# Attention with a mixture of experts on one core: the second sweep's first expert takes its last chunk after both groups, and GpSimd scales half of the weights

## The chip, the core and the metric

One of the eight cores of a Trainium2 chip runs the whole program. The metric is the device time of one execution in microseconds: 979.92 us for the kernel before (median of three, 979.89 to 981.65).

## What is computed

Causal attention with a decay (4 batches, 8 heads, 576 tokens, head size 64) makes x, 2304 tokens by 512. Four experts of two layers (512 to 1024 to 512) then run on every token and are summed with normalised weights p. All of it is in float32.

```python
scores = q @ k.T / 8 + cum[:, None] - cum[None, :]   # cum: running sum of log f; causal
x = softmax(scores) @ v                              # per head, joined to [2304, 512]
out = sum(p[:, e:e+1] * (relu(x @ w1[e]) @ w2[e]) for e in range(4))
```

## The kernel before

**Work.** Tokens are cut into nine chunks of 256. Each expert has eight slabs of 128 hidden features; a slab holds a piece of the first layer's weights (columns 0 to 511 of a tile) and of the second layer's (512 to 1023). A group g is half an expert, four slabs; a step (s, g, c, ps) is two of its slabs on one chunk in one sweep: 24 matmuls of 128x256 in `l1` (L859), a gate, and 12 of 128x512 in `l2` (L891), whose sums end in `gather` (L910, L914). Every value is split into a high and a low part and three products are added.

**Sweeps.** `SWEEPS` lists the chunks of each expert. The first sweep takes what attention has finished early. The second, in float16 pairs, takes chunks 1, 2, 3, 4 for experts 0 and 1, chunks 2 to 4 for expert 2 and 3 to 4 for expert 3: steps 28 to 79 of 80. Chunks 5 to 8 come last, in the class `Big`. In a sweep the groups come one after the other, and a group does all its chunks before the next group starts.

**Attention in between.** The heads of attention are 64 (pair of heads, half of the tokens): `qk_pe` (s, L540), `qk_min` and `qk_exp`, `tr_pe` (t, L632), `av_pe` (o, L682), `spread` (b, L600). They are issued in small pieces between the parts of the steps. `marks` and `pace` spread them by estimated costs so that a chunk is there `LEAD` steps before the first step that uses it; if it isn't, `upto(need[cur.c])` issues all that is missing at once. Chunk 4 needs all the heads of batch 0's second half. Before a chunk's first step in the second sweep, `x_scale` finds its largest value (xmax, L253, then topx on PE, L192 and L213), and `narrow` makes its float16 pair y (L411 on ACT, L412 on DVE).

**Weights.** `w_load` brings a slab into one of three tiles wr. `w_split` makes the pair of a slab in the second sweep: for each half k, ACT scales and rounds (L826) and DVE subtracts (L827). It is called when a group's last chunk releases two slabs, and splits the two that lie six slabs ahead (L1259 to L1262). In the second sweep there is room for twelve slabs. Each pair is also stored for later (wd). `w_peek` reads the next expert's weights for their largest value, one piece a step (pk, L277).

**Order.** Below the startup a scheduler fixes the order of each engine's instructions when the program is built; each engine runs its list in order and waits where an input is late. POOL (GpSimd) also makes pieces of q and k of every head (L488, L496, L502) and spreads the reciprocals (rb, L590).

Of the kernel before, what the change touches and what calls it, by code (L numbers as in the profile page):

```python
# [12 lines left out]
AF = mybir.ActivationFunctionType  # L13
ALU = mybir.AluOpType
# [11 lines left out]
SWEEPS = (  # L26
    ((0,), (0,), (0, 1), (0, 1, 2)),
    ((1, 2, 3, 4), (1, 2, 3, 4), (2, 3, 4), (3, 4)),
)
# [5 lines left out]
LAST = (5, 6, 7, 8)  # L35
# [40 lines left out]
def fused(ctx: ExitStack, tc: tile.TileContext, qk, v, f, probs, w, out):  # L76
    nc = tc.nc
# [105 lines left out]
    def at_step(n, f):  # L183
        later.setdefault(n, []).append(f)
# [47 lines left out]
    def behind(f):  # L232
        if prev is None:
            f()
            return
        with tc.issue_after(prev.last.ins):
            f()
# [32 lines left out]
    def w_peek(e, i):  # L270

        n, k = divmod(i, 2)
        t = pk_p.tile([128, 512], F32, tag="pk", name=f"pk{e}_{i}")
        nc.sync.dma_start(out=t, in_=w[8 * e + n, :, 512 * k : 512 * k + 512])
        at_step(
            step + 1,
            lambda: nc.vector.tensor_reduce(  # L277
                out=wmax[:, k, n, e : e + 1], in_=t, op=ALU.max, axis=AX.X, apply_absolute_value=True
            ),
        )  # L280
# [57 lines left out]
    def weigh(e, c):  # L338

        k = min(c, LAST[0])  # L340
        if (e, k) in weighed:
            return
        weighed.add((e, k))
        assert ("w", e) in known and ("x", k) in known
        o = slice(2 * c, 2 * c + 2) if c < LAST[0] else slice(2 * LAST[0], 2 * LAST[-1] + 2)
        nc.gpsimd.tensor_scalar(
            out=scg[:, e, o],
            in0=prob[:, o, e],
            scalar1=wun[:, e : e + 1],
            scalar2=xun[:, k : k + 1],  # L350
            op0=ALU.mult,
            op1=ALU.mult,
        )
# [52 lines left out]
    def narrow(c):  # L406

        y_tiles(c)
        sc = xsc[:, c : c + 1]
        x = xh[c].bitcast(F32) if c in WIDE else xf[c]  # L410
        nc.scalar.activation(out=yh[c], in_=x, func=AF.Copy, scale=sc)  # L411
        nc.vector.scalar_tensor_tensor(  # L412
            out=yl[c], in0=x, scalar=sc, in1=yh[c], op0=ALU.mult, op1=ALU.subtract
        )
        if c in WIDE:
            nc.vector.scalar_tensor_tensor(
                out=yl[c], in0=xl[c].bitcast(F32), scalar=sc, in1=yl[c], op0=ALU.mult, op1=ALU.add
            )
# [364 lines left out]
    wh, wl, wraw = {}, {}, {}  # L783
    NS = len(SWEEPS) * E * (FF // 128)

    def w_load(n):
        if n < NS and n not in wraw:
            wraw[n] = wr_p.tile([128, 1024], F32, tag="wr", name=f"wr{n}")
            nc.sync.dma_start(out=wraw[n], in_=w[n % 32])
# [3 lines left out]
    def w_pair(name):  # L793
        t = w_p.tile([128, 2, 1024], F16, tag=("wh", "wl")[len(pairs) % 2], name=name)
        pairs.append(t)
        return t

    def w_split(n):
        if n >= NS:
            if n % 2 == 0:  # L800
                big_split((n - NS) // 2)
            return
        w_load(n)
        r = wraw.pop(n)
        if n < 32:
            wh[n] = w_p.tile([128, 1024], F32R, tag="wh", name=f"wh{n}")
            wl[n] = w_p.tile([128, 1024], F32R, tag="wl", name=f"wl{n}")
            nc.scalar.activation(out=wh[n], in_=r, func=AF.Copy)
            eng = nc.vector if n in W_DVE else nc.gpsimd
            for a in (0, 512):  # L810
                z = a + 512
                eng.tensor_tensor(
                    out=wl[n][:, a:z],
                    in0=r[:, a:z],
                    in1=wh[n][:, a:z].bitcast(F32),
                    op=ALU.subtract,
                )
        else:
            e = n % 32 // 8
            assert ("w", e) in known  # L820
            t = w_pair(f"w{n}")
            wh[n], wl[n] = t[:, 0], t[:, 1]
            for k in range(2):
                c = slice(512 * k, 512 * k + 512)
                sc = wsc[:, e, k : k + 1]
                nc.scalar.activation(out=wh[n][:, c], in_=r[:, c], func=AF.Copy, scale=sc)  # L826
                nc.vector.scalar_tensor_tensor(  # L827
                    out=wl[n][:, c],
                    in0=r[:, c],
                    scalar=sc,  # L830
                    in1=wh[n][:, c],
                    op0=ALU.mult,
                    op1=ALU.subtract,
                )
            at_step(step + 2, lambda: nc.sync.dma_start(out=wd[n - 32], in_=t))
        w_load(n + 1)
        w_load(n + 2)
        w_load(n + 3)
# [141 lines left out]
    def big_split(p):  # L980
        if p >= 16:
            return
        r = wr_p.tile([128, 2, 512], F32, tag="wr", name=f"wr{NS + p}")
        nc.sync.dma_start(
            out=r, in_=w[2 * p : 2 * p + 2, :, :512].rearrange("n p c -> p n c")
        )
        bw[p] = [w_pair(f"bw{p}_{k}") for k in range(3)]
        for k in range(2):
            nc.sync.dma_start(out=bw[p][k], in_=wd[2 * p + k])
        part = lambda b: r[:, b[0], 256 * b[1] : 256 * b[1] + 256]  # L990
        t = late.x.tile([128, 4, 256], F32, tag="wt", name=f"wt{p}", bufs=2)
        w_of = lambda b: part(b) if type(b) is tuple else t[:, b - 1, :]
        for k, a, z, op in SUMS:
            nc.gpsimd.tensor_tensor(out=t[:, k - 1, :], in0=w_of(a), in1=w_of(z), op=op)  # L994
        f = t.rearrange("p k n -> p (k n)")
        hi, lo = bw[p][2][:, 0], bw[p][2][:, 1]
        nc.scalar.activation(out=f, in_=f, func=AF.Copy, scale=wsc[:, p // 4, 0:1])
        nc.scalar.activation(out=hi, in_=f, func=AF.Copy)  # L998
        for a in (0, 512):
            z = a + 512  # L1000
            nc.gpsimd.tensor_tensor(out=lo[:, a:z], in0=f[:, a:z], in1=hi[:, a:z], op=ALU.subtract)  # L1001

    class Big:
# [81 lines left out]
    steps = [  # L1085
        Step(s, g, c, ps)
        for s, sets in enumerate(SWEEPS)
        for g in range(8)
        for c in sets[g // 2]
        for ps in range(2)  # L1090
    ]

    done_at = {}
    for n, (j, _) in enumerate(heads):
# [37 lines left out]
    def upto(n):  # L1132
        nonlocal at
        while at < n:
            asteps[at][1]()
            at += 1
# [14 lines left out]
    def pace(n):  # L1151
        for (n0, c0), (n1, c1) in zip(marks, marks[1:]):
            if n <= n1:
                goal = c0 + (c1 - c0) * (n - n0) / (n1 - n0)
                break
        else:
            goal = cost[-1]
        m = at
        while m < len(asteps) and cost[m + 1] <= goal:
            m += 1  # L1160
        upto(m)
# [45 lines left out]
    prev, step = None, 0  # L1207
# [13 lines left out]
    for n in range(len(steps) + 1):  # L1221
        step = n
        cur = steps[n] if n < len(steps) else None
        for f_ in later.pop(n, ()):
            behind(f_)
        for e, first_ in enumerate(PEEK):
            if 0 <= n - first_ < 16:
                w_peek(e, n - first_)
            if n == first_ + 17:
                a_, b_ = w_scale(e)  # L1230
                behind(a_)
                at_step(n + 3, b_)
        if cur is not None:
            if cur.c not in used:
                used.add(cur.c)
                upto(need[cur.c])
            for c, m in TURN:
                if n >= m and c not in yh and ("x", c) in known:
                    narrow(c)
            if cur.s == 1:  # L1240
                assert cur.c in yh
                weigh(cur.g // 2, cur.c)
            for q in range(4):
                cur.l1(q)
                pace(n + q / 8)
            cur.gate()
        else:
            upto(len(asteps))
            chunks.close()
            late.h = late.enter_context(tc.tile_pool(name="h", bufs=8, side="right"))  # L1250
            for e in range(E):
                weigh(e, LAST[0])
            big = [Big(p) for p in range(16)]
            big[0].l1()
        if prev is not None:
            for q in range(4):
                prev.l2(q)
                pace(n + (q + 4) / 8)
            if prev.c == SWEEPS[prev.s][prev.g // 2][-1]:  # L1259
                base = prev.w0 + 6  # L1260
                w_split(base)
                w_split(base + 1)  # L1262
        prev = cur

    for p in range(16):
# [49 lines left out]
```

## Time and profile before

| what | us |
|---|---|
| median of three | 979.92 |
| the profiled execution, its own time | 980.82 |
| its span, first to last instruction | 978.6 |
| PE busy | 944.8 |
| DVE, ACT, POOL busy | 709.4, 471.0, 341.9 |

The span is what the profile covers; the profiled execution's own time is 2.2 us longer than it and 0.9 us above the median. PE is the matrix engine, DVE the vector engine, ACT the scalar engine, POOL GpSimd, SP the queue that issues the transfers. A busy PE need not be a PE at its full rate. The second sweep runs from about 238 to 661 us.

### The profile page before, as it was taken

The numbers are of one execution on the slowest core, as the hardware profiler recorded it, in microseconds if no ns is written. First come the engines' busy times: TensorE is split into PE (matmuls) and PEld (weight loads), VectorE is DVE, ScalarE is ACT, GpSimd is POOL, SyncE is SP. The second block draws the span as 40 slices with busy tenths as digits, with TensorE's granted clock in tenths as the row PEclk, the third lists the DMA queues.
The fourth block names the chain that finished last, engine by engine and source line by source line (L and its number), as shares of the span: only waits on it lengthen the run. The fifth ranks groups of instructions, "written<-read, shape, count | busy, mean of one in ns | idle before, by whom it ended". The sixth has DMA issues, their size and how long they took to land.

```text
span 978.6 us, 15658 instructions
## 1 busy us (share of the span) xinstructions
PE 944.8 (97%) x5695; PEld 647.8 (66%) x5695; DVE 709.4 (72%) x1485; ACT 471.0 (48%) x931; POOL 341.9 (35%) x400
## 2 busy tenths in 40 slices
PE   5799999999997999999999999999999999999998
PEld 4699999898765877777777777764444444444443
DVE  5768767877878897677966785568766766676665
ACT  6767465466467765446745564364222322231110
POOL 4766776343133422213222121386224223320000
PEclk9999999999999899999999999999999999999999
DMA  6456644485623293333922192044222312121002
GB/s 220 138 167 220 221 148 149 127 285 194 225 79 103 78 398 111 95 108 123 388 90 62 56 365 74 28 151 151 86 65 86 108 66 79 51 65 44 0 1 86
DMA packets 49772, 129.41 MB, mean 132 GB/s; under 512 B 5700, under 2 KB 8320, under 8 KB 49696
## 3 DMA queue, kind: packets, MB, share of 16 engines
q1 hardware_dynamic: 49696, 128.42, 38.6%
q8 instruction: 45, 0.74, 0.3%
q14 instruction: 31, 0.25, 0.1%
HBM read 106.75 MB, written 21.65 MB: 131 GB/s over the span
## 4 chain that ended last, share of the span: by engine, by line
PE 83%; DVE 5%; POOL 4%; DMA 3%; ACT 3%; issue 2%; SPq 0%; ACTq 0%; POOLq 0%; DVEq 0%
PE l L859 19%; PE l L891 18%; PE y L1074 17%; PE m L1016 14%; PE s L540 5%; PE t L632 5%; PE o L682 5%; DMA raw<-in_qk 1%; POOL wt L994 1%; DMA wr<-in_w 1%; POOL bw L1001 1%; PE b L600 1%; POOL rx L974 1%; DVE p L554 1%; DMA pk<-in_w 1%
## 5 line engine op out<-in xcount | busy, mean ns | idle before, releaser
L859 PE MATMUL l<-y,w 128*128 128x256 f16 x1248 | 162.4, 273 | 0.6 <-DVE y L412 0.6
L1074 PE MATMUL y<-bw,hh 128*128 128x512 f16 x512 | 151.8, 379 | 1.3 <-ACT hh L1042 1.3
L1016 PE MATMUL m<-rh,bw 128*128 128x512 f16 x448 | 139.1, 379 | 0.4 <-ACT rh L975 0.4
L569 ACT ACTIVATE p<-p,nm 128x576 f32<-128x576 f32 (+2 forms) x160 | 96.0, 600 | 88.2 <-DVE nm L554 87.6
L859 PEld LDWEIGHTS <-w 128*128 128x128 f16 x1248 | 117.4, 98 | 29.1 <-issue 6.8
L914 DVE SCALAR_TENSOR_TENSOR acc<-y,scg,acc 128x512 f32<-128x512 f32 x120 | 89.4, 749 | 59.8 <-PE y L1074 59.0
L891 PE MATMUL l<-w,gh 128*128 128x512 f16 x416 | 126.5, 380 | 1.4 <-ACT gh L872 0.9
L1016 PEld LDWEIGHTS <-bw 128*128 128x128 f16 x672 | 65.8, 98 | 79.6 <-issue 0.7
L488 POOL CAST q<-raw 64x320 fp32r<-64x320 f32 (+1 forms) x56 | 24.9, 445 | 266.6 <-PE s L540 203.8
L1001 POOL TENSOR_TENSOR bw<-wt,bw 128x512 f16<-128x512 f32 x32 | 37.2, 1184 | 174.0 <-ACT bw L998 174.0
L1074 PE MATMUL y<-bw,hl 128*128 128x512 f16 x256 | 96.5, 379 | 0.0
L554 DVE CUSTOM_DVE_ANT_0 p<-s,mask 128x288 f32<-128x288 f32 (+2 forms) x160 | 75.5, 477 | 23.8 <-PE s L540 22.9
L540 PE MATMUL s<-hi 128*128 128x384 f32 (+1 forms) x192 | 77.2, 405 | 15.2 <-DVE hi L502 8.8
L1074 PEld LDWEIGHTS <-hh 128*128 128x128 f16 x512 | 50.0, 98 | 62.0 <-ACT hh L1042 1.8
L632 PE MATMUL t<-ident,p 128*128 128x128 f32 x480 | 86.2, 287 | 4.1 <-ACT p L569 3.9
L1033 DVE TENSOR_TENSOR u<-m,u 128x512 f32<-128x512 f32 x96 | 65.6, 689 | 28.0 <-PE m L1016 27.0
L649 DVE TENSOR_TENSOR ptl<-t,pth 128x320 fp32r<-128x320 f32 (+2 forms) x120 | 65.5, 552 | 27.6 <-ACT pth L642 27.0
L1016 PE MATMUL m<-rl,bw 128*128 128x512 f16 x224 | 84.9, 379 | 0.0
L642 ACT ACTIVATE pth<-t 128x384 fp32r<-128x384 f32 (+2 forms) x120 | 58.0, 498 | 43.0 <-PE t L632 38.8
L891 PE MATMUL l<-w,gl 128*128 128x512 f16 x208 | 78.4, 379 | 0.0
L873 DVE SCALAR_TENSOR_TENSOR gl<-l,gh 128x512 f16<-128x512 f32 (+1 forms) x80 | 54.8, 686 | 30.4 <-ACT gh L872 29.9
L1042 ACT ACTIVATE hh<-u 128x512 f16<-128x512 f32 x64 | 39.5, 627 | 76.5 <-DVE u L1033 76.4
(136 smaller groups left out, 2069.8 us busy)
## 6 DMA issues: line engine op xcount, KB each, us to landing
wr<-in_w SPq DMA_DIRECT2D x80, 512.0 KB
pk<-in_w SPq DMA_DIRECT2D x64, 256.0 KB
wd<-w SPq DMA_DIRECT2D x32, 512.0 KB
bw<-wd SPq DMA_DIRECT2D x32, 512.0 KB
raw<-in_qk SPq DMA_DIRECT2D x16, 896.0 KB
raw<-in_qk SPq DMA_DIRECT2D x12, 512.0 KB
vr<-in_v SPq DMA_DIRECT2D x16, 320.0 KB
out<-acc SPq DMA_DIRECT2D x16, 256.0 KB
```

The source lines that it names most:

```text
L540: nc.tensor.matmul(out=ps[:, at : at + z - a], lhsT=lhsT, rhs=rhs, start=(m == 0), stop=(m == 1),)
L554: nc.vector.tensor_tensor_reduce(out=pt[:, a:z], in0=ps, in1=mask[:, m0 + a : m0 + z], scale=-0.125, scalar=BIG if n == 0 else nm[:, col : ...
L569: nc.scalar.activation(out=pt[:, :w_], in_=pt[:, :w_], func=AF.Exp, scale=-1.0, bias=self.nmax[hh][:, c : c + 1], accum_out=self.ssum[:, h ...
L632: nc.tensor.transpose(ps[:, at : at + 128], self.p[hh, it][:, TOK0[jt] : TOK0[jt] + 128], ident)
L642: nc.scalar.activation(out=self.pt[hh][0][:, a0 : a0 + at - first], in_=ps[:, first:at], func=AF.Copy)
L649: nc.vector.tensor_tensor(out=lo[:, a0 + first : a0 + at - first], in0=ps[:, 2 * first : at], in1=hi[:, a0 + first : a0 + at - first].bitc ...
L859: nc.tensor.matmul(out=self.l1p[:, fi, :], lhsT=lhsT, rhs=rhs[:, k, :], start=(k == 0 and m == 0), stop=(k == 3 and m == 2),)
L891: nc.tensor.matmul(out=l2[tt], lhsT=lhsT, rhs=rhs, start=(self.ps == 0 and fi == 0 and m == 0), stop=(self.ps == 1 and fi == 1 and m == 2),)
L914: nc.vector.scalar_tensor_tensor(out=acc[c][:, tt, :], in0=ps, scalar=sc, in1=acc[c][:, tt, :], op0=ALU.mult, op1=ALU.add,)
L1016: nc.tensor.matmul(out=ps, lhsT=lhsT[:, o], rhs=rhs[:, k, :], start=(k == 0 and i == 0), stop=(k == 1 and i == 2),)
L1033: nc.vector.tensor_tensor(out=out, in0=a, in1=z, op=op)
L1074: nc.tensor.matmul(out=ps, lhsT=lhsT, rhs=rhs, start=(fi == 0 and m == 0), stop=(fi == 1 and m == 2),)
```

## The change

Two edits. The order of the steps: group 0 of the second sweep's first expert leaves out chunk 4, group 1 does chunks 1, 2 and 3, and then group 0 and group 1 do chunk 4. The table `ends` says which step now triggers which `w_split`, so that the slabs of both groups stay. And in the second sweep the second layer's half (k = 1) of each slab is scaled in place by POOL, rounded by ACT and subtracted by POOL; DVE no longer touches it.

```diff
             for k in range(2):
                 c = slice(512 * k, 512 * k + 512)
                 sc = wsc[:, e, k : k + 1]
+                if k == 1:
+                    nc.gpsimd.tensor_scalar(
+                        out=r[:, c], in0=r[:, c], scalar1=sc, scalar2=None, op0=ALU.mult
+                    )
+                    nc.scalar.activation(out=wh[n][:, c], in_=r[:, c], func=AF.Copy)
+                    nc.gpsimd.tensor_tensor(
+                        out=wl[n][:, c], in0=r[:, c], in1=wh[n][:, c], op=ALU.subtract
+                    )
+                    continue
                 nc.scalar.activation(out=wh[n][:, c], in_=r[:, c], func=AF.Copy, scale=sc)
...
+    behind_1 = [t for t in steps if (t.s, t.g, t.c) == (1, 0, LAST[0] - 1)]
+    for t in behind_1:
+        steps.remove(t)
+    at_1 = next(n for n, t in enumerate(steps) if (t.s, t.g, t.c) == (1, 1, LAST[0] - 1))
+    steps[at_1:at_1] = behind_1
+    ends = {
+        t.w0: t for t in steps if t.c == SWEEPS[t.s][t.g // 2][-1] and t not in behind_1
+    }
+    for t in steps:
+        if t.s == 1 and t.c == LAST[0] - 2 and (t.g, t.ps) in ((0, 0), (1, 0)):
+            ends[32 + 2 * t.g] = t
...
-            if prev.c == SWEEPS[prev.s][prev.g // 2][-1]:
-                base = prev.w0 + 6
-                w_split(base)
-                w_split(base + 1)
+            for w0, t in ends.items():
+                if t is prev:
+                    w_split(w0 + 6)
+                    w_split(w0 + 7)
```

The order, as the scheduler leaves it. In a name such as l2_1_0_3_0_1 stand sweep, group, chunk, ps and the token half; in s0_2_1_0_3_0 batch, pair of heads, half, head, tile. The last number of a name is a buffer's.

PE, before, where group 0 ends with chunk 3:

```order
L891 MATMUL l2_1_0_3_0_1_4311<-w35_3755,gl1_0_3_1_4293 128x512
L632 MATMUL t0_1_1_1_0_3225<-ident_111,p0_1_1_1_4_3020 128x128
L632 MATMUL t0_1_1_1_0_3225<-ident_111,p0_1_1_1_3_3019 128x128
L632 MATMUL t0_1_1_1_0_3225<-ident_111,p0_1_1_1_4_3020 128x128
L632 MATMUL t0_1_1_1_1_3262<-ident_111,p0_1_1_1_4_3020 128x128
L632 MATMUL t0_1_1_1_1_3262<-ident_111,p0_1_1_1_2_3018 128x128
L632 MATMUL t0_1_1_1_1_3262<-ident_111,p0_1_1_1_3_3019 128x128
L632 MATMUL t0_1_1_1_1_3262<-ident_111,p0_1_1_1_4_3020 128x128
L540 MATMUL s0_2_1_0_3_0_3277<-hi0_2_1_0_3025 128x512
L540 MATMUL s0_2_1_0_3_0_3277<-kl0_2_1_0_2863,q2_0_113 128x512
```

From there to the first matmul of chunk 4 the list holds 188 matmuls, all of them attention's.

PE, with the change, at the same place:

```order
L900 MATMUL l2_1_0_3_0_1_4309<-w35_3753,gl1_0_3_1_4294 128x512
L868 LDWEIGHTS w38_4324
L868 MATMUL l1_1_1_1_1_4419<-y1_2362,w38_4324 128x256
L540 MATMUL s0_2_1_1_4_0_3514<-hi0_2_1_1_3206 128x288
L540 MATMUL s0_2_1_1_4_0_3514<-kl0_2_1_1_3036,q2_1_114 128x288
L868 LDWEIGHTS w38_4324
L868 MATMUL l1_1_1_1_1_4419<-y1_2362,w38_4324 128x256
```

Group 1 goes on behind group 0's last row, and attention's rows stand between its own.

PE, with the change, where group 1 ends with chunk 3:

```order
L900 MATMUL l2_1_1_3_0_1_4853<-w39_4332,gh1_1_3_1_4837 128x512
L900 LDWEIGHTS gh1_1_3_1_4837
L900 MATMUL l2_1_1_3_0_1_4853<-w39_4332,gh1_1_3_1_4837 128x512
L900 LDWEIGHTS gl1_1_3_1_4838
L900 MATMUL l2_1_1_3_0_1_4853<-w39_4332,gl1_1_3_1_4838 128x512
L540 MATMUL s1_0_1_1_3_0_4182<-hi1_0_1_1_3911 128x512
L540 MATMUL s1_0_1_1_3_0_4182<-kl1_0_1_1_3723,q2_1_114 128x512
L213 MATMUL topx4_172<-ux4_173,ones_r_126 128x1
```

From the last l2 row to the first matmul of chunk 4 the list now holds 32 matmuls.

POOL, before, from the reciprocals of one pair of heads to those of the last pair that chunk 4 needs (rb0_3_1):

```order
L590 COPY rb0_2_1_3509<-rs0_2_1_3181 128x384
L488 CAST q2_0_113<-raw1_0_1_3552 64x320
L496 TENSOR_TENSOR kl1_0_1_0_3550<-raw1_0_1_3552,hi1_0_1_0_3708 64x576
L502 TENSOR_TENSOR hi1_0_1_0_3708<-raw1_0_1_3552,hi1_0_1_0_3708 64x320
L488 CAST q2_1_114<-raw1_0_1_3552 64x320
L496 TENSOR_TENSOR kl1_0_1_1_3713<-raw1_0_1_3552,hi1_0_1_1_3893 64x576
L502 TENSOR_TENSOR hi1_0_1_1_3893<-raw1_0_1_3552,hi1_0_1_1_3893 64x320
L590 COPY rb0_3_1_3839<-rs0_3_1_3544 128x384
```

POOL, with the change, the end of the same stretch:

```order
L488 CAST q2_0_113<-raw1_0_1_3561 64x320
L831 TENSOR_TENSOR w42_5236<-wr42_4338,w42_5236 128x512
L496 TENSOR_TENSOR kl1_0_1_0_3559<-raw1_0_1_3561,hi1_0_1_0_3718 64x576
L502 TENSOR_TENSOR hi1_0_1_0_3718<-raw1_0_1_3561,hi1_0_1_0_3718 64x320
L827 TENSOR_SCALAR wr43_4872<-wr43_4872,wsc_120 128x512
L827 TENSOR_SCALAR wr44_4880<-wr44_4880,wsc_120 128x512
L831 TENSOR_TENSOR w43_5244<-wr43_4872,w43_5244 128x512
L827 TENSOR_SCALAR wr45_5242<-wr45_5242,wsc_120 128x512
L488 CAST q2_1_114<-raw1_0_1_3561 64x320
L496 TENSOR_TENSOR kl1_0_1_1_3723<-raw1_0_1_3561,hi1_0_1_1_3911 64x576
L502 TENSOR_TENSOR hi1_0_1_1_3911<-raw1_0_1_3561,hi1_0_1_1_3911 64x320
L590 COPY rb0_3_1_3877<-rs0_3_1_3553 128x384
```

Between head pieces of q and k now stand pieces of the weights (wr, w), and rb0_3_1 is behind them.

## Rows read from the trace of the kernel before

**Rows 1.** The page: PE over the whole span, and the granted clock in 40 slices.

```profile
PE 944.8 (97%) x5695; PEld 647.8 (66%) x5695; DVE 709.4 (72%) x1485; ACT 471.0 (48%) x931; POOL 341.9 (35%) x400
...
PEclk9999999999999899999999999999999999999999
```

**Rows 2.** Windows: span, busy us of each engine (instructions), granted clock, DMA share, GB/s.

```profile
285.20:328.90 43.70, 34.77 (x198) 27.42 (x197) 35.13 (x104) 33.21 (x72) 19.18 (x22) 0.92 0.27 87
...
315.90:328.90 13.00, 10.02 (x47) 8.46 (x48) 9.77 (x31) 9.96 (x21) 7.30 (x8) 0.74 0.12 30
...
237.90:328.90 91.00, 82.07 (x523) 62.34 (x523) 74.00 (x194) 59.81 (x125) 30.39 (x35) 0.96 0.38 128
...
328.90:656.00 327.10, 326.92 (x2321) 244.11 (x2321) 241.99 (x556) 180.39 (x358) 91.96 (x108) 1.00 0.44 155
...
340.00:620.00 280.00, 279.83 (x1988) 210.26 (x1986) 211.38 (x493) 157.96 (x321) 62.91 (x72) 1.00 0.47 167
```

**Rows 3.** Windows, the same columns, four microseconds each.

```profile
316.00:320.00 4.00, 1.66 (x12) 1.61 (x12) 3.66 (x8) 2.93 (x5) 2.04 (x2) 0.92 0.00 0
...
320.00:324.00 4.00, 4.00 (x15) 3.12 (x14) 3.48 (x15) 2.29 (x7) 1.25 (x3) 0.50 0.26 82
```

**Rows 4.** Timeline of PE: start, us, instruction, count, [idle before <- releaser].

```profile
315.34 0.55 PE L600 MATMUL b<-ident,rb 128*128 128x128 f32 x3
...
318.34 0.27 PE L192 MATMUL topx<-ident,xmax 128*1 128x128 f32 x1 [2.45 <-DVE xmax L253]
...
328.92 2.78 PE L859 MATMUL l<-y,w 128*128 128x256 f16 x24 [0.56 <-DVE y L412]
```

**Rows 5.** Lines by form, PE, 340 to 620 us: count | busy us, mean ns.

```profile
L859 PE MATMUL l<-y,w 128*128 128x256 f16 x912 | 119.6, 273 | 0.0
...
L891 PE MATMUL l<-w,gh 128*128 128x512 f16 x296 | 90.1, 380 | 0.0
...
L891 PE MATMUL l<-w,gl 128*128 128x512 f16 x149 | 56.4, 379 | 0.0
```

**Rows 6.** Chain that ended last, two merged pieces: start us, us, what.

```profile
340.05 2.62 PE l L859 x24
...
349.74 1.29 PE l L891 x6
```

**Rows 7.** Timeline of DVE around the wait for chunk 4.

```profile
317.07 1.21 DVE L253 TENSOR_REDUCE xmax<-xf 128x1 f32<-128x1024 f32 x1
...
326.76 0.56 DVE L554 CUSTOM_DVE_ANT_0 p<-s,mask 128x384 f32<-128x384 f32 x1 [2.17 <-PE s L540]
...
327.62 1.25 DVE L412 SCALAR_TENSOR_TENSOR y<-xf,xsc,y 128x1024 f16<-128x1024 f32 x1
```

**Rows 8.** Lines by form, DVE, whole span.

```profile
L277 DVE TENSOR_REDUCE wmax<-pk 128x1 f32<-128x512 f32 x64 | 43.4, 678 | 13.2 <-DMA pk<-in_w 13.2
...
L873 DVE SCALAR_TENSOR_TENSOR gl<-l,gh 128x512 f16<-128x512 f32 x52 | 35.6, 686 | 16.6 <-ACT gh L872 16.3
...
L914 DVE SCALAR_TENSOR_TENSOR acc<-l,scg,acc 128x512 f32<-128x512 f32 x48 | 35.5, 744 | 2.8 <-PE l L891 2.6
```

**Rows 9.** One line at a time, L826 and L827: count, duration min/median/max, starts.

```profile
L826 ACT ACTIVATE w<-wr,wsc x64: 705/709/723, 202.4 to 581.3; 128x512 f16<-128x512 f32 x64
...
L827 DVE SCALAR_TENSOR_TENSOR w<-wr,wsc,w x64: 700/746/1521, 204.3 to 582.7; 128x512 f16<-128x512 f32 x64
```

**Rows 10.** Lines by form, POOL, whole span.

```profile
L1001 POOL TENSOR_TENSOR bw<-wt,bw 128x512 f16<-128x512 f32 x32 | 37.2, 1184 | 174.0 <-ACT bw L998 174.0
...
L488 POOL CAST q<-raw 64x320 fp32r<-64x320 f32 x32 | 14.5, 452 | 231.3 <-PE s L540 180.5 <-DMA raw<-in_qk 19.6 <-DMA pk<-in_w 13.8
...
L590 POOL COPY rb<-rs 128x384 f32<-128x384 f32 x16 | 11.4, 710 | 34.1 <-DVE rs L588 33.8
```

**Rows 11.** One line, L976: the same DVE form beside a busy POOL.

```profile
L976 DVE SCALAR_TENSOR_TENSOR rl<-rx,xsc,rh x8: 740/1342/1724, 647.0 to 665.8; 128x512 f16<-128x512 f32 x8
```

**Rows 12.** Waits, whole span: us in total, times, longest us.

```profile
POOL q L488 <- PE s L540: 208.7, 30, 18.9
```

## The prediction

> **What bounds the kernel now.** I read the page's first table first: PE is busy 944.8 of 978.6 us [rows 1]. What it has to do doesn't change, so a gain can only come from the 34 us in which it stands, or from time in which it is busy but slow. Part of these lie at the program's start and end, where the change moves nothing. The granted clock, in the same rows, drops once in the middle, so there I asked for windows. From 285.2 to 328.9 us PE is busy 34.8 of 43.7 us, and the next 327 us have no hole [rows 2]. The hole is the wait for chunk 4: between the last l2 row of chunk 3 and the first l1 row of chunk 4 the order has 188 matmuls of attention and nothing of the experts. It ends with 2.45 us in which PE waits for the chunk's largest value, and 0.56 us in which it waits for y [rows 4]. In 316 to 324 us the granted clock is 0.92 and then 0.50, the lower of its two levels (1.2 of 2.4 GHz) [rows 3], right behind that idle time. Then comes the DVE timeline: the y of chunk 4 is the end of a line of small DVE instructions that starts at the xmax of 317.07 [rows 7].
>
> **First part: the order of the steps.** Nothing is added on PE; six steps move from behind chunk 4 to before it.
>
> What is a packed microsecond worth? In 340 to 620 us PE is full and mixes both kinds of work. An l1 matmul takes 2.62/24 = 0.109 us and an l2 matmul 1.29/6 = 0.215 us in the chain [rows 6]. The 912 and 445 of them [rows 5] take 99.4 + 95.7 = 195.1 us, so the other 1988 - 1357 = 631 matmuls [rows 2] get 84.9 us, 0.135 us each. The hole holds 198, two of them l1: 196 x 0.135 + 0.2 = 26.6 us if packed. It takes 43.7. So **17.1 us** are lost there: the idle time, the low clock, and ends of matmuls that nothing overlaps.
>
> How much of it comes back? A step is 24 x 0.109 + 12 x 0.215 = 5.2 us, six are 31.2 us, more than the hole needs. But they don't reach its end. In the new order, behind the last b rows of chunk 4's heads, there remain 5 l1, 24 l2 and 43 small matmuls: 0.5 + 5.2 + 5.8 = 11.5 us. In the trace it takes 13.0 us from there to y, with DVE busy 9.8 [rows 2]. DVE's list in the changed order has four instructions more in that stretch, a gl, a pk and two acc: 0.69 + 0.68 + 2 x 0.74 = 2.9 us [rows 8]. If DVE's waits stay, y comes after 15.9 us; the largest, 2.17 us for a score matmul [rows 7], fell into the slow clock, and with 1 us of waits in all it is 13.6. So PE still waits 2.1 to 4.4 us for chunk 4; I take **3.2**. I expect no drop of the clock, since l2 rows now stand where PE idled 2.45 us.
>
> Then the density. From the sweep's start to chunk 4 the time becomes 91.0 - 17.1 + 31.2 + 5.2 = 110.3 us (3.2 for chunk 4, and 2 for what this paragraph says). DVE's work there goes from 74.0 us [rows 2] up by six gl, six acc and six pk (4.1 + 4.5 + 4.1), by the first halves of six more slabs (6 x 0.746 = 4.5 [rows 9]) and down by four second halves (3.0): 88.2 us, or 80%. That is DVE's share in the hole (35.1 of 43.7), where head waited for head; in 340 to 620 us it is 75% and PE doesn't wait. I allow **2 us** for short waits, between nothing and the 7 us of the first rival. Behind chunk 4, 40 steps instead of 46 carry the same heads, and DVE has about 207 us of work in 296, 70% (242 less six steps' 12.7, less 4.5 of halves done earlier, less 24 second halves' 17.9), against 74% before. No hole opens there by DVE.
>
> **Second part: half of the weights on POOL.** Removed: 32 DVE subtractions of 0.746 us, 24 us. DVE isn't on the path outside of the hole, so this alone is worth nothing; in the hole it is the 3.0 us above. ACT keeps its 32 instructions of 0.71 us. Added: 32 subtractions on POOL, whose nearest row is bw, the same shape and types, 1.18 us; and 32 scalings with one tensor input. The trace has none of this size. Below, the cast of 64x320 takes 0.45 us and longer rows can't take less; above, the two-input row takes 1.18; the copy of 128x384 takes 0.71 [rows 10], and by its columns 512 make 0.95, which I take. That is 2.1 us a slab, 68 us of POOL in all. POOL is busy 92.0 of 327.1 us behind chunk 4 [rows 2]; with 20 slabs 134 of 296. What hides it: weights are split two or more steps (10 us) before their use, against about 3 us for POOL, ACT, POOL. If that cover goes, PE waits in l2. Queued behind POOL's new rows are the pieces of q and k and rb0_3_1, on which the next score matmuls and chunk 4 wait. A tile wr is held longer by these 2 us, so loads and stores on SP start later by as much; I cost that at nothing while PE's steps lie further ahead.
>
> **The sum.** 17.1 - 3.2 - 2.0 = 11.9 us. The profiled execution would go from 980.8 to 968.9; taken from the median, 979.9 to **968.0 us**.
>
> **Rivals.** *DVE and POOL hold each other up.* The weight subtraction takes 0.746 us in the middle [rows 9], and the same form beside a busy POOL 1.342 [rows 11], 0.6 more. Ten first halves before chunk 4 would add 6 us: DVE 94.2 us. If 80% is all that this mix lets DVE do, the stretch takes 94.2/0.80 = 117.7 instead of 122.2 us (91.0 + 31.2): a gain of 4.5, **975.4 us**. For it: the hole ran at just that share. Against: there the heads were alone, and later 75% went with a full PE. The Trainium skill, "SBUF — State Buffer", section "Who interferes with whom", says that a VectorE instruction with two SBUF inputs contends with a GpSimd instruction that reads SBUF; the L976 row agrees, and by that rule this rival comes true where the two meet.
>
> *Everything packs.* y comes early and no wait is left: 16 to 17.1 us, **963.5 us**. Against: y's line on DVE gets longer by 2.9 us.
>
> *POOL's queue stops PE: slower.* POOL works in order and already waits 208.7 us for score matmuls [rows 12]. Where a weight piece waits for its ACT rounding or its load, the q and k pieces behind it come late, and PE's own order has their score matmuls at fixed places. The gain is gone once each of 32 slabs costs PE 0.37 us, 3 us per expert. At 5 us per expert it is 20 - 11.9 = 8 us slower, **988 us**. For it: the rows of w42 to w45 among those of head 1_0. Against: POOL is under half busy and PE has 13 us per head.
>
> *The order doesn't change what waits* (979.9): the new order itself speaks against it, 32 rows instead of 188.
>
> **Chances.** Forecast 0.56, DVE with POOL 0.24, all packed 0.10, POOL's queue 0.08, no change 0.02. About eight in ten of these lie between 963.5 and 976.5, with the bounds of the two waits (2.1 to 4.4, 0 to 7) inside. A difference of 0.2%, 2 us, is about what a measurement of this kernel can tell from none. Faster by more: the first three without the far end of the second, 0.87. Slower: 0.08. The rest, 0.05, is the same.
>
> **What would show it.** Right: l2 and l1 rows among attention's between chunk 3 of group 0 and chunk 4; no window at half clock there; 2 to 5 us of PE idle before the first l1 of chunk 4, released by DVE; no new idle in the 296 us behind it; second halves at 0.7 on ACT, 1.2 and about 0.95 on POOL. Wrong: PE waiting for kl, hi or rb from POOL, or an l2 waiting for w; L836 (the old L827) at 1.3 us; or a hole at chunk 4 as long as the six steps that were moved.

## The result and the profile after

The changed kernel takes **970.11 us** (median, 968.61 to 970.36) against 980.05 of the kernel before, run beside it: a ratio of 0.9889 [0.9876, 0.9903], 9.9 us faster. The forecast was 968.0 with a range of 963.5 to 976.5. The profiled execution took 970.31 us, span 968.5; that of before 980.8 and 978.6.

The page, with the rows that answer to [rows 1]:

```profile
span 968.5 us, 15684 instructions
...
PE 937.9 (97%) x5695; PEld 642.6 (66%) x5695; DVE 698.4 (72%) x1453; ACT 469.6 (48%) x931; POOL 429.3 (44%) x464
...
PEclk9599999999999999999999999999999999999999
```

DVE has its 32 instructions fewer, POOL 64 more and 87 us more of work. The dip of the clock in the middle is gone. Windows of the changed kernel, as [rows 2]:

```profile
238.00:345.60 107.60, 106.02 (x739) 79.86 (x739) 88.20 (x216) 66.40 (x136) 55.47 (x56) 1.00 0.48 162
...
345.60:640.00 294.40, 291.79 (x2066) 219.12 (x2066) 212.35 (x500) 170.10 (x342) 134.09 (x133) 0.99 0.47 152
580.00:584.00 4.00, 1.69 (x14) 1.30 (x13) 2.67 (x7) 3.35 (x7) 4.00 (x4) 0.93 0.98 386
584.00:588.00 4.00, 4.00 (x23) 2.95 (x22) 1.84 (x6) 1.93 (x6) 2.56 (x4) 0.65 0.84 278
```

From the sweep's start to chunk 4, PE now idles 1.6 us instead of the 8.9 that stood there before [rows 2], and never at the lower clock. The last two rows are new: a hole at 580 us and a low clock behind it, where the kernel before had none. PE's timeline with the change at the sweep's first l1, at both places, and at the last row where the two programs still differ:

```profile
237.99 2.79 PE L868 MATMUL l<-y,w 128*128 128x256 f16 x24
...
330.83 0.54 PE L600 MATMUL b<-ident,rb 128*128 128x128 f32 x3
...
335.21 0.27 PE L192 MATMUL topx<-ident,xmax 128*1 128x128 f32 x1
...
340.45 0.40 PE L540 MATMUL s<-hi 128*128 128x288 f32 x1 [0.37 <-DVE nm L554]
...
345.65 2.78 PE L868 MATMUL l<-y,w 128*128 128x256 f16 x24 [1.07 <-DVE y L412]
...
583.60 0.90 PE L632 MATMUL t<-ident,p 128*128 128x128 f32 x3 [2.31 <-ACT p L569]
...
646.62 0.59 PE L900 MATMUL l<-w,gh 128*128 128x512 f16 x2 [0.55 <-DVE acc L923]
```

And the first and the last of these rows before:

```profile
237.90 2.79 PE L859 MATMUL l<-y,w 128*128 128x256 f16 x24
...
656.70 0.59 PE L891 MATMUL l<-w,gh 128*128 128x512 f16 x2 [0.54 <-DVE acc L914]
```

Against [rows 4], topx waits for nothing: l1 and l2 rows stand between it and the b rows, and before y there is 1.07 us of idle time. The last row was at 656.70 before, so 10.1 us are gained there, and nothing changes behind it. Two differences tell where. From the sweep's first f16 l1 (237.90 before, 237.99 now) to the first l1 of chunk 4 that waits for y, it was 91.0 us and, with six steps more (31.2 us by the prediction's working), 122.2; it is 107.7 now: **14.6 us gained**. From there to that last row it was 327.8, without the six steps 296.6; it is 301.0 now: **4.4 us lost**. Their sum is measured; how it splits rests on the 31.2 us, an estimate from the rows of before.

The chain of waits through the new hole (start us, us, what):

```profile
564.94 1.17 POOL w L831
...
566.12 4.88 DMA wr<-in_w
...
571.79 1.15 DVE w L836
...
574.02 0.67 DVE acc L923
...
574.71 0.34 SPq L933
...
575.13 4.33 DMA wr<-in_w
...
579.49 0.73 ACT w L835
...
582.68 0.88 ACT p L569 x2
...
583.60 0.48 PE t L632
```

Two slabs of the last expert arrive late one after the other. The first one's tile is one of three, and comes free (566.1) only after POOL's scaling and subtraction of an earlier slab; the subtraction of that slab's own first half on DVE (571.79) then stands ahead of acc. The second one's tile is free once POOL's next subtraction is done, at 572.4:

```profile
571.23 1.16 POOL L831 TENSOR_TENSOR w<-wr,w 128x512 f16<-128x512 f32 x1
```

But its load stands on SP's queue behind a final store (L933) that waits for acc, and is issued 2.7 us later, at 575.13. The ACT and DVE instructions of this slab stand ahead of attention's p on their engines, and PE waits for p. The new instructions by line, as [rows 9, 10]:

```profile
L827 POOL TENSOR_SCALAR wr<-wr,wsc x32: 1552/1563/2383, 194.7 to 579.7; 128x512 f32<-128x512 f32 x32
...
L831 POOL TENSOR_TENSOR w<-wr,w x32: 1147/1161/1615, 205.9 to 585.1; 128x512 f16<-128x512 f32 x32
```

POOL's scaling takes 1.56 us, longer than the subtraction with its two inputs.

### The profile page after: what moved, and what is told of

Its sections match the earlier page's. It is cut to its first block, busy times and chain, and to the rows that moved or that the text cites. A ratio compares the mean times of both kernels' runs of the same rounds, so it can differ in the third digit from the quotient of the medians.

```text
span 968.5 us, 15684 instructions
## 1 busy us (share of the span) xinstructions
PE 937.9 (97%) x5695; PEld 642.6 (66%) x5695; DVE 698.4 (72%) x1453; ACT 469.6 (48%) x931; POOL 429.3 (44%) x464
## 4 chain that ended last, share of the span: by engine, by line
PE 75%; POOL 7%; DVE 7%; DMA 6%; ACT 3%; issue 2%; SPq 0%; POOLq 0%; DVEq 0%; ACTq 0%
PE y L1083 17%; PE l L868 16%; PE l L900 15%; PE m L1025 14%; PE s L540 5%; PE t L632 4%; PE o L682 4%; DMA wr<-in_w 2%; POOL wt L1003 1%; DMA pk<-in_w 1%; POOL wr L827 1%; DMA raw<-in_qk 1%; POOL w L831 1%; DVE p L554 1%; POOL bw L1010 1%
## 5 line engine op out<-in xcount | busy, mean ns | idle before, releaser
L868 PE MATMUL l<-y,w 128*128 128x256 f16 x1248 | 169.5, 274 | 1.1 <-DVE y L412 1.1
L540 PE MATMUL s<-hi 128*128 128x384 f32 (+1 forms) x192 | 76.9, 403 | 12.7 <-DVE hi L502 8.8
L1025 PE MATMUL m<-rl,bw 128*128 128x512 f16 x224 | 84.9, 379 | 0.0
```

Of the source, the lines that this page charges most:

```text
L540: nc.tensor.matmul(out=ps[:, at : at + z - a], lhsT=lhsT, rhs=rhs, start=(m == 0), stop=(m == 1),)
L868: nc.tensor.matmul(out=self.l1p[:, fi, :], lhsT=lhsT, rhs=rhs[:, k, :], start=(k == 0 and m == 0), stop=(k == 3 and m == 2),)
L1025: nc.tensor.matmul(out=ps, lhsT=lhsT[:, o], rhs=rhs[:, k, :], start=(k == 0 and i == 0), stop=(k == 1 and i == 2),)
```

## The experiments

All runs are read in one way. T2 - T1 is the time from the sweep's first f16 l1 to the first l1 of chunk 4 behind y, E - T2 from there to the last row that differs (the l2 behind acc), both from PE's timeline. "Idle" is what PE's busy time leaves open in windows of 4 us, "slow" its busy time times one minus the granted clock, both first before T2 and then behind it. The two runs in the old order have six steps (31.2 us) behind T2 instead of before it. Each ratio is to the kernel before as it ran beside that kernel (medians 980.0 to 981.0).

| kernel | T2 - T1 | E - T2 | idle before, behind | slow before, behind | profiled us | median us | ratio [95%] |
|---|---|---|---|---|---|---|---|
| before (old order) | 91.0 | 327.8 | 8.9, 0.7 | 3.3, 0 | 980.8 | 980.05 | 1 |
| the change | 107.7 | 301.0 | 1.6, 3.1 | 0, 1.2 | 970.3 | 970.1 | 0.9889 [0.9876, 0.9903] |
| order alone | 113.5 | 304.7 | 4.7, 5.1 | 1.7, 1.5 | 980.1 | 977.1 | 0.9967 [0.9954, 0.9979] |
| GpSimd's half alone (old order) | 85.4 | 330.0 | 8.4, 0.8 | 0, 0 | 978.2 | 976.7 | 0.9967 [0.9953, 0.998] |
| GpSimd for expert 0 | 109.1 | 303.3 | 2.4, 4.2 | 0, 1.5 | 974.9 | 974.0 | 0.9926 [0.9906, 0.9946] |
| GpSimd for experts 1 to 3 | 110.9 | 304.0 | 3.7, 3.8 | 4.1, 1.5 | 976.9 | 974.2 | 0.9943 [0.9928, 0.9957] |
| GpSimd for experts 0 to 2 | 108.8 | 297.1 | 2.2, 0.8 | 0, 0 | 968.0 | 967.1 | 0.9866 [0.9851, 0.9882] |
| ScalarE scales, all experts | 109.8 | 297.6 | 3.4, 1.3 | 0, 0 | 971.6 | 972.6 | 0.9921 [0.9906, 0.9936] |
| ScalarE rounds first, all | 110.7 | 298.8 | 3.7, 2.3 | 0, 0 | 972.1 | 970.5 | 0.9893 [0.9877, 0.991] |
| ScalarE rounds first, DVE for expert 3 | 109.9 | 298.6 | 3.1, 1.4 | 0, 0 | 969.2 | 970.2 | 0.9892 [0.9875, 0.9909] |
| ScalarE scales expert 3 | 108.5 | 297.3 | 2.0, 0.9 | 0, 0 | 967.3 | **965.5** | 0.9845 [0.9826, 0.9863] |
| ScalarE scales experts 1 to 3 | 108.5 | 297.5 | 1.9, 1.2 | 0, 0 | 968.2 | 968.7 | 0.9883 [0.9869, 0.9898] |
| store on ScalarE's queue | 107.4 | 297.9 | 1.6, 1.4 | 0, 0 | 967.8 | 967.4 | 0.9869 [0.9857, 0.9882] |

Three things must be known to read the table.

- T2 is a place in PE's list, and the scheduler makes that list anew for each kernel. In the new order 739 or 740 matmuls lie between T1 and T2, but 725 with GpSimd for experts 1 to 3; in the old order 524, but 507 with GpSimd's half alone. The 14 and the 17 that are missing, nearly all of attention, lie behind T2 there. At the prediction's 0.135 us each they are about 1.9 and 2.3 us, an estimate, which belong in the first column: like for like it is 112.8 and 302.1 us for the one kernel, 87.7 and 327.7 for the other.
- The stretches are those of the one profiled execution, whose own time the table gives. With the order alone it was the longest of twelve (974.5 to 980.1 us) and 3.0 us above their median, with GpSimd for experts 1 to 3 the longest of six and 2.7 us above. What these two kernels lose by the table is more than their medians show.
- From T1 to E, what is left after idle and slow time is 405.9 us before and 401.8 to 406.2 in all the others. PE has the same matmuls in all of them, and most of the difference lies in where it waits; some 4 us of spread are in neither of these columns.

T1 itself moves, between 236.98 and 240.51 us. PE's timelines of before, the change and the order alone list the first sweep's rows in different orders; whether that is what moves T1 wasn't tested. ScalarE scaling for all experts has the latest T1, 2.5 us behind the change's, which is why its profiled execution is 1.3 us longer than the change's although its two stretches together are 1.2 us shorter.

**The two parts alone.** The order without the second part:

```diff
-                if k == 1:
+                if False:
```

> The new order of the steps alone; DVE splits both halves of the weights as before. Theory (the order gives all of the gain, about 14.5 us up to chunk 4, and GpSimd's half costs about 4 us near 580 us, where PE stood 2.3 us and the clock fell behind it): 965.7 us, no PE idle near 580 us. Rival (the stretch before chunk 4 needs DVE relieved, so GpSimd's half is part of the gain): 970 us or more, with PE idle growing before chunk 4.

And GpSimd's half without the order: the kernel before, with the change's block for k == 1 in `w_split`.

> GpSimd's half alone, the steps in the old order. Theory: the hole before chunk 4 stays at 43 to 44 us and the stall near the last expert's weights appears: 982 to 984 us. Rival (GpSimd's half shortens the hole, since DVE is its bound): 975 to 978 us, hole under 41 us.

By their medians each alone gains 3 us, together they gain 10. Of both expectations the theory missed and the rival's time held. PE's timeline with the order alone:

```profile
338.80 0.55 PE L600 MATMUL b<-ident,rb 128*128 128x128 f32 x3
...
341.80 0.27 PE L192 MATMUL topx<-ident,xmax 128*1 128x128 f32 x1 [2.45 <-DVE xmax L253]
...
351.67 2.78 PE L868 MATMUL l<-y,w 128*128 128x256 f16 x24 [1.10 <-DVE y L412]
...
388.92 0.45 PE L540 MATMUL s<-hi 128*128 128x384 f32 x1 [1.69 <-DVE nm L554]
...
457.62 0.40 PE L540 MATMUL s<-hi 128*128 128x288 f32 x1 [1.00 <-DVE ptl L649]
...
466.97 0.66 PE L632 MATMUL t<-ident,p 128*128 128x128 f32 x4 [0.62 <-DVE xs L704]
```

The order does move PE's work into the hole: the stretch is 113.5 instead of 122.2 us, 8.7 gained. But topx stands directly behind the b rows again, as before, PE idles 2.45 us for xmax, and the clock falls behind it (0.78 in 344 to 348 us). In the change 18 l2 and 5 l1 rows stand between the two. These rows sort the waits at topx in all thirteen kernels:

| between the last b row and topx | kernels | PE's wait for xmax, us |
|---|---|---|
| nothing | before, order alone, GpSimd's half alone, GpSimd for experts 1 to 3 | 2.45, 2.45, 2.45, 3.67 |
| 12 l2 | ScalarE scales, all | 1.85 |
| 15 l2 | ScalarE rounds first (both), GpSimd for expert 0 | 1.48, 0.94, 0.23 |
| 18 l2 and 5 l1, or 19 l2 | the change and the four others | none |

So this wait hangs mostly on what PE's list has left for that place. xmax itself doesn't come later with the order alone than before: topx starts 3.0 us behind the start of the b rows in both. Nor does DVE's work alone set the list: where ScalarE scales, or rounds first, for all experts, DVE is relieved as in the change, and only 12 and 15 rows are left. What makes the scheduler leave more or fewer wasn't followed, and DVE's split wasn't tried with PE's list of the change.

In this execution 8.1 us are lost behind chunk 4, where PE now waits for DVE five times, for 0.4 to 1.7 us; three of these waits are shown. The chain to the first:

```profile
377.85 9.87 DMA pk<-in_w
...
388.35 0.51 DVE p L554
```

Here DVE itself is idle for 4.27 us until a piece for `w_peek` has landed, and attention's p stands behind that. The chain to the last of the three:

```profile
444.74 4.42 DVE w L836 x4
...
449.16 0.47 DVE p L554
...
450.02 10.38 DMA wr<-in_w
...
464.01 2.38 DVE w L836 x2
...
466.42 0.51 DVE xs L704
```

Weight subtractions of two slabs stand in a row on DVE, the load behind them goes out late, and attention's p and xs come behind further subtractions. DVE's share over that stretch says nothing of this: behind chunk 4 DVE is 74% busy with the order alone, and 74% before. What counts is that it is late at single places.

GpSimd's half alone makes the old hole shorter by 5.7 us in the table (85.4 for 91.0), but 2.3 of these are the 17 matmuls that moved behind T2, and the stretch behind is 2.3 us longer for it. That leaves 3.4 us. PE still waits for xmax as long as before, but without the half clock of [rows 3], the 3.3 us of slow time:

```profile
318.26 0.27 PE L192 MATMUL topx<-ident,xmax 128*1 128x128 f32 x1 [2.45 <-DVE xmax L253]
```

Before chunk 4 the two parts give 8.7 + 3.4 = 12.1 of the 14.6 us; 2.5 come only when both are there. In the new order the second part is worth 5.8 us in that stretch (113.5 to 107.7), in the old one 3.4.

**Which slabs.** The last expert's second halves back on DVE:

```diff
-                if k == 1:
+                if k == 1 and e < 3:
```

> The changed kernel, but the last expert's eight slabs (w56 to w63) are split by DVE alone, as before. Theory (the loss behind chunk 4 comes from that expert's slabs on GpSimd): 966 us, 300.97 us from the first l1 of chunk 4 to the last step's l2 become about 297. Rival (the loss is anywhere behind chunk 4, from tighter packing of six steps fewer): 970 us, the stall near 580 us stays.

967.1 us: the hole at 580 us is gone, and E - T2 is 297.1, half a microsecond from the 296.6 of a full PE. The window of that run:

```profile
580.00:600.00 20.00, 20.00 (x151) 15.65 (x149) 11.22 (x30) 8.35 (x20) 2.76 (x3) 1.00 0.15 54
```

Then the first expert alone (`e == 0` in that line), and the other three alone (`e > 0`).

> GpSimd takes the slabs of the first expert alone; VectorE the other three. Theory A (the relief of VectorE is worth something in two places: 14.6 us gained before chunk 4 instead of 8.7, which hangs on the first expert's slabs, and 8.1 us lost behind chunk 4 without it, which hangs on those of experts 1 to 3): gain before chunk 4 stays 13 to 15 us, the loss behind it is 6 to 8 us as in the order alone, time 972 to 975. Rival (the loss behind chunk 4 belongs to the order, and the first expert's slabs alone took it away): 966 to 968.

> The other half of the run in which GpSimd takes the first expert alone: here VectorE takes the first expert's slabs and GpSimd those of experts 1 to 3. Theory A (two separate effects: the first expert's slabs set the gain before chunk 4, the other three the loss behind it): first f16 product of sweep 2 to first of chunk 4 about 113 us as in the order alone (109 with GpSimd on the first expert), loss behind chunk 4 at most 4.4 us as in the change, so 973 to 975. Rival (relief of VectorE before chunk 4 is worth nothing, the 113.5 of the order alone was chance): 107.5 to 110 us there and 969 to 971.

For the first expert alone, theory A's time held (974.0): 13.1 us gained before chunk 4 and 6.7 lost behind it, in the waits that the order alone had too. Its PE timeline:

```profile
385.20 0.44 PE L540 MATMUL s<-hi 128*128 128x384 f32 x1 [1.81 <-DVE nm L554]
...
453.92 0.40 PE L540 MATMUL s<-hi 128*128 128x288 f32 x1 [0.98 <-DVE ptl L649]
```

The run before this one, with GpSimd for experts 0 to 2, differs from it in experts 1 and 2 alone, and has neither wait: they belong to the slabs of these two.

For experts 1 to 3 theory A's time held as well (974.2). T2 - T1 lies between the two theories in the table (110.9), and at theory A's 113 like for like (112.8); 5.5 us are lost behind it, not at most 4.4. The two waits above are gone here too. The wait for ACT's p is back, with 2.4 us at 590 us. And PE waits longer than ever for xmax, with nothing between the b rows and topx, and falls to the lower clock:

```profile
340.73 0.37 PE L192 MATMUL topx<-ident,xmax 128*1 128x128 f32 x1 [3.67 <-DVE xmax L253]
```

The window behind it, of the same run:

```profile
340.00:344.00 4.00, 3.27 (x14) 2.85 (x14) 2.59 (x8) 1.15 (x3) 0.00 (x0) 0.50 0.27 82
```

Idle and slow time before chunk 4 are 7.8 us, against 1.6 in the change, and like for like the stretch is 5.1 us longer: so much hangs there on who splits the first expert's slabs. By the table of the waits at topx it comes at least in part through PE's list; no subtraction stands on DVE in the 6 us before that wait ends.

**What the hole at 580 us is made of.** ScalarE scales in place instead of GpSimd, for all experts:

```diff
-                    nc.gpsimd.tensor_scalar(
-                        out=r[:, c], in0=r[:, c], scalar1=sc, scalar2=None, op0=ALU.mult
-                    )
+                    nc.scalar.activation(out=r[:, c], in_=r[:, c], func=AF.Copy, scale=sc)
```

> The changed kernel, but ACT scales the second half in place (about 0.7 us) and GpSimd only subtracts; GpSimd's 1.56 us scaling goes. Theory (the slabs' tiles come free late because of GpSimd's 1.56 and 1.16 us in a row, so loads and with them ACT's queue are late): the stall near 580 us shrinks, 966 to 967 us. Rival (loads are late because the SP queue waits for other things): 970 us, the same stall.

The theory's stall is gone, with GpSimd still subtracting for every expert, but not its time. The stretch before chunk 4 is 2.1 us worse than the change's, with 1.85 us of idle time at topx, where 12 l2 rows are left, and the late T1 is on top. Next, ScalarE rounds from the raw slab before GpSimd scales it, so that it doesn't wait for GpSimd (the second run has `k == 1 and e < 3` in the first line, so DVE takes expert 3):

```diff
                 if k == 1:
+                    nc.scalar.activation(out=wh[n][:, c], in_=r[:, c], func=AF.Copy, scale=sc)
...
-                    nc.scalar.activation(out=wh[n][:, c], in_=r[:, c], func=AF.Copy)
```

> ScalarE rounds the high half straight from the loaded slab with the scale in its own instruction, so it no longer waits for GpSimd; GpSimd then scales the slab in place and subtracts, for all four experts. Theory A (the stall at 580-584 us of the changed kernel comes from the two GpSimd instructions, 1.56 and 1.16 us each, that hold a slab's tile until its low half is taken, with one tile fewer free than loads want): GpSimd's work and the tile's time are as before, the stall with the last expert stays at 1.5 to 3 us, time 969 to 971. Theory B (the stall comes from ScalarE standing in its queue behind GpSimd's scaling): the stall goes, 966 to 967.

> As the run in which VectorE takes the last expert's slabs (967.1), but ScalarE rounds straight from the loaded slab for the first three. If ScalarE's wait for GpSimd costs TensorE anything in the first three experts, 965 to 966; if the only stall was that of the last expert, 967 as there (within 0.5).

Both missed. With all experts the hole at 580 us went, as theory B had it (20.00 of 20 us busy from 580), but not the time: 970.5. A new wait stands at 478 us, and the chain to it shows how:

```profile
459.81 1.57 POOL wr L828
...
461.77 1.13 POOL w L831
462.90 1.38 POOL kl L496
...
464.35 1.21 POOL hi L502
...
465.63 1.16 POOL w L831
...
466.79 0.41 POOL rb L590
...
467.20 7.60 DMA raw<-in_qk
...
477.68 0.51 DVE xs L704
```

Attention's kl and hi stand behind a slab's two instructions on POOL, and rb behind one more. By the chain the load of the next head's q and k goes out only then, and PE waits 1.56 us for xs. So GpSimd's order can stop PE by a second way, that of the third rival. With DVE for expert 3 as well it was 970.2: its two stretches are 1.1 and 1.5 us longer than in the run where GpSimd scales first for the same three experts. Taking ScalarE's wait for GpSimd away gained nothing there. Then the remedy that shortens GpSimd's part instead: for expert 3, ScalarE scales and rounds, GpSimd only subtracts; and the same for experts 1 to 3 (`e == 0` in place of `e < 3`).

```diff
-                if k == 1:
+                if k == 1 and e < 3:
...
+                if k == 1:
+                    nc.scalar.activation(out=r[:, c], in_=r[:, c], func=AF.Copy, scale=sc)
+                    nc.scalar.activation(out=wh[n][:, c], in_=r[:, c], func=AF.Copy)
+                    nc.gpsimd.tensor_tensor(
+                        out=wl[n][:, c], in0=r[:, c], in1=wh[n][:, c], op=ALU.subtract
+                    )
+                    continue
```

> Last expert alone: ScalarE scales the slab in place (0.7 us) and rounds it, GpSimd only subtracts (1.16 us instead of 1.56 + 1.16); experts 0 to 2 as in the change. Theory A (length of GpSimd's two steps per slab makes the last expert's stall): no stall at 580-584 us, 966 to 968. Theory C (any use of GpSimd for the last expert stalls it, since its queue also takes other work there): stall of 1.5 us or more, 969 to 971.

> As the run in which ScalarE scales the last expert's slabs in place and GpSimd only subtracts there (965.5), with that form for experts 1 to 3; GpSimd scales for the first expert alone. If GpSimd's 1.56 us for scaling still costs something behind chunk 4 in experts 1 and 2: 964 to 965.3. If what is left there is not GpSimd's: 965.5 within 1. If ScalarE, with 1.3 us more for each of 16 slabs, becomes late: 967 or more.

The first gave **965.5 us**, the lowest median of all: no hole near 580, 2.8 us of idle time in the 406 us from T1 to E. Its ratio to before, 0.9845 [0.9826, 0.9863], lies below the change's without overlap; from DVE for expert 3 (0.9866) and from the store's run (0.9869) the intervals don't tell it apart, and the profiled executions of these three lie within 0.8 us. In the second nothing was left behind chunk 4 for it to win (1.2 us idle against 0.9), and 968.7 is the number of the third case without its reason: no wait for ScalarE above 0.2 us shows on PE. The two profiled executions are 0.9 us apart, 0.75 of it by T1. The rest of the 3 us of difference in the medians is in executions without a profile and stays open: the first kernel's profiled execution was 1.8 us above its median, the second's 0.4 below.

Last, the store. Only the final stores of the chunk that ends with the third expert leave SP's queue:

```diff
-                nc.sync.dma_start(out=out[r0 : r0 + n, :], in_=acc[c][o : o + n, tt, :])
+                q_ = nc.scalar if c == 2 else nc.sync
+                q_.dma_start(out=out[r0 : r0 + n, :], in_=acc[c][o : o + n, tt, :])
```

> The changed kernel with one thing else: the final stores of the chunk that is done with the third expert go out from ScalarE's queue instead of SP's, so that the load of the last weight slab stands behind no store. Theory A (the 2.3 us stall at 583.6 us of the changed kernel is that load, held for 2.7 us behind the store on SP's queue): the load is issued when its tile comes free, the stall goes, 967 to 968.5. Theory B (the store is beside the point: GpSimd's late release of the slab's tile and the 4 us of the load make the stall): stall of 1.5 us or more stays, 969.5 to 971. Theory C (ScalarE now waits for the store's data instead): the stall moves to another wait for ScalarE, 969 to 972.

967.4 us, theory A's time. SP's queue and PE in that run:

```profile
572.89 0.33 SPq L789 DMA_DIRECT2D wr<-in_w  x1
...
583.24 0.55 PE L632 MATMUL t<-ident,p 128*128 128x128 f32 x3 [0.89 <-ACT p L569]
```

The last slab's load is issued at 572.89 instead of 575.13, and the wait falls from 2.31 to 0.89 us. So 1.4 of the 2.3 us go with the store in front of the load. What remains is the other part, on ACT:

```profile
581.80 0.63 ACT L830 ACTIVATE w<-wr 128x512 f16<-128x512 f32 x1 [0.99 <-POOL wr L827]
582.33 0.76 ACT L569 ACTIVATE p<-p,nm 128x576 f32<-128x576 f32 x1
```

ACT stands 0.99 us for GpSimd's scaling, with attention's p behind it. How early the last slab's load is issued, counted back from E, sorts all the runs: 83 to 87 us where DVE takes expert 3 (84.9 before the change, 571.79 to 656.70), 79 to 80 where ScalarE scales and GpSimd subtracts, 71 to 76 where GpSimd does both (71.5 in the change, 575.13 to 646.62). Only among the five kernels of the last kind does PE wait there, and not in all (2.3 us in the change, 2.4 with GpSimd for experts 1 to 3, 0.9 here, none in two). The two long waits are in the two kernels in which that load stands directly behind L933 on SP's queue. So the lead is short in all five, and what stands on SP's, POOL's and ACT's queues at that moment decides whether PE feels it. A fourth tile for the slabs wasn't tried.

## Why the prediction was right, and where not

Time, sign and main mechanism held: forecast 968.0, measured 970.1, inside the range and 2 us above the forecast. l2 rows stand where PE idled. In the new order, the two experiments whose list has none there show that wait and the low clock again. Two terms were off, in opposite directions.

- **The hole's worth, 17.1 us.** Held: idle and slow time before chunk 4 fell from 12.2 to 1.6 us, 10.6 of the 14.6 us that came back; the other 4.0 are in neither, where the term also counted ends of matmuls that nothing overlaps.
- **The residual wait of 3.2 us and 2 us of short waits.** Too large: 1.07 us before y, 0.37 before a score matmul, and 17.1 - 14.6 = 2.5 us for both terms together, not 5.2. That isn't because y came earlier: from the end of the last b rows (331.37) to y's first l1 it takes 14.3 us, against the 13.6 assumed. PE had more to do there: it is busy for 12.7 of them, where the working had 11.5. Most of that is its count: the timeline has 7 l1, 26 l2 and 45 small matmuls there, not 5, 24 and 43. The term is the difference of the two: its time for DVE's line was slightly too small, and its time for PE's rows too small by more. No drop of the clock, as expected.
- **DVE's load.** The working gave 88.2 us for the stretch; the window shows 88.20, which is 82% with PE full. In part that is luck: eight first halves (L836) ran there and not ten, and they took 1.09 us each on average, where L827 took 0.78 in the same stretch before. So 80% isn't the most that this mix lets DVE do, and the first rival falls, though its contention is there, 2.5 us in all instead of 6, and PE didn't feel it. It is not beside every POOL instruction: of the nine L836 that lie by themselves in the timeline beside POOL's scaling alone, seven took 0.74 to 0.78 us; beside POOL's subtraction of two inputs there are 1.19 (at 358.98) and 1.55 (at 248.28). The rise agrees with the rule that was cited for it (the Trainium skill, "SBUF — State Buffer", section "Who interferes with whom"); but that rule has any GpSimd instruction that reads SBUF, and the scaling, which reads it too, mostly cost nothing here.
- **"DVE isn't on the path outside of the hole, so this alone is worth nothing."** This step failed. The order alone gains 3.0 us, with the second part 9.9. Before chunk 4 the second part is worth 5.8 us in the new order; the 3.0 of the working are near what it gives in the old one (3.4). Behind chunk 4 the order alone loses 8.1 us in its profiled execution, at single late places of a DVE that is 74% busy, two of whose waits go with the subtractions of experts 1 and 2. "No hole opens there by DVE" came true only because of the second part, and the argument for it, a share of busy time, was wrong. What is not shown is how much of this is DVE's time itself and how much the list that the scheduler makes for a busier DVE.
- **Loads and stores on SP later, "at nothing".** This step failed too: 4.4 us are lost behind chunk 4, most of it at the hole at 580 us and the low clock behind that. Moving one store, or relieving GpSimd in the last expert, brings all but 0.5 to 1.3 us of it back. The working held for the first three experts (0.5 us lost where DVE takes the last) and failed with the last, whose load is late.
- **POOL's scaling, 0.95 us between 0.45 and 1.18.** Out of its bounds: 1.56 us, so 2.7 us a slab and not 2.1. "Longer rows can't take less" than a cast held; that one input is never dearer than two did not.
- **POOL's queue (third rival).** The mechanism exists, at one expert and not at four: 2.3 us in the changed kernel, through ACT and a late load rather than through kl and hi. The way through kl and hi showed up in an experiment.

The two misses nearly cancel (2.7 us more gained before chunk 4 than the 11.9 forecast, 4.4 lost behind it where nothing was), which is luck; the range was wide enough for either alone.

## What to carry to other kernels

Moving work into a hole takes it from the stretch that had hidden something else: look for what that stretch's other engine has in a row, since its mean share (70 to 74% here) doesn't tell whether it comes too late. Where a scheduler makes each engine's list, an edit to one engine's work also moves the rows of the others: compare the lists before a difference is put down to the edit itself. When an in-place step on a slower engine holds a buffer of a small rotating pool, its cost isn't its duration but the lead that each later load loses, and the loss shows where the lead runs out, here with the last of four experts. Treat the engine split as a choice per stage: three experts by GpSimd and the last by VectorE or with ScalarE's help gave 967.1 and 965.5 us, where one rule for all gave 970.1.

## What was not expected of the hardware

- GpSimd's scaling of 128x512 f32 by a column of scalars, in place, takes 1.56 us and its two-input subtraction of the same size 1.16. The Trainium skill ("GPSIMD Engine Reference", section "Engine selection") has one-input work at roughly line rate and two-input work about twice as slow as VectorE; here the one with a single tensor input is the slower, by 0.4 us, and the measurement decides.
- In this profiled execution the granted clock was at its lower level in the program's second fortieth (0.50 in 28 to 48 us), and it cost nothing: the sweep began at 237.99 us, against 237.90 before without it.
- With GpSimd's half alone, PE idles the same 2.45 us at topx as before, but the clock stays at 1.00 behind it, where it fell to 0.50 before and in the run with 3.67 us. So the length of this wait doesn't settle it by itself; what does wasn't followed further.
